# Moving the conversion of W_out between pairs of feed-forward steps

## The chip, the cores and the metric

The kernel runs on one core of a Trainium2 chip. The metric is the device time of one execution in microseconds (us). An engine is one of TensorE (PE, matmuls, with its weight loads shown apart as PEld), VectorE (DVE), ScalarE (ACT), GpSimd (POOL) and SyncE (SP, which issues nearly all DMAs). Each engine works through its own list of instructions in order and waits for the others at semaphores.

## The reference

Attention with a hashed mask, then a gated feed-forward; all in float32. Only the second half matters here.

```python
# attention: scores kept where the 6-bit hash buckets of query and key agree, softmax, times v
x = attn_out.transpose(0, 2, 1, 3).reshape(3072, 512)
h = x @ w_in                            # 3072 x 2048
g = h * (1.0 / (1.0 + np.exp(-1.702 * h)))
out = g @ w_out                         # 3072 x 512
```

The two weight matrices come to the kernel as 64-bit floats, so each is loaded as pairs of 32-bit words and turned into float32 on the chip ("converted").

## The kernel before, in words

**The work.** After the attention, `feed_forward` computes g for three blocks of 1024 tokens (the change's title calls a block a "token"; here it is "block 0, 1, 2") and writes g and sums of it to memory (`g_dram`); then it reads them back and multiplies by W_out. Both products are made by Strassen-Winograd recursion: seven products in place of eight, with sums on DVE and POOL. The first product has 8 steps per block, numbered n = 0 to 23, n = 8 * block + step. Steps 2 to 19 are taken in pairs t = 1 to 9 (`NESTED`), with n = 2t and 2t + 1. Pair 3 is the last of block 0, pairs 4 to 7 are block 1, pairs 8 and 9 are block 2.

**One pair.** `pair_of_steps` writes out the order by hand. PE runs ten full products of four matmuls of 512 columns (`product`, L743; p1, p6, p7, p5, p4, each for the first and the second step of the pair) and fourteen small ones of two matmuls of 256 columns (`small`, L817), two of the seven products being split a second time. The small ones are numbered go1, go6, go2, go7, go5, go4, go3, as their `go(i)` has it. PE's order in a pair is:

```
p1(0) go6' go2'  p1(1) go7'  p6(0) go5'  p6(1) go4'  p5(0) go3'
go1  p7(0) go6 go2  p7(1) go7  p5(1) go5  p4(0) go4  p4(1) go3   go1'
```

The marked ones belong to the split product 3, whose last six are carried over into the next pair. Small products use two places in PSUM: go1, go6, go7, go4 all go to place "a", go2, go5, go3 to place "x" (pool `inner`, one buffer each). DVE adds each result out of its place into u or v (L753, `u<-small` or `v<-small`), and PE may not write a place again before that. So go3 waits for DVE's addition of go5, go1' for that of go4, and go6' for that of go1'.

**What is put between.** `hook(1)` to `hook(10)` are places in that order where other work is issued: hook 6 stands ahead of p7(1), hook 7 ahead of p5(1), hook 8 ahead of p4(0), hook 9 ahead of p4(1), hook 10 at the end of the pair. `places_of` lists, for the two steps of a pair, the hooks that take their pieces of work; what is left over goes to hook 5 or 10.

**A conversion.** W_out comes in 16 chunks of 512 KB. `convert` does one chunk: a DMA into `raw` (L162, one buffer), then six DVE instructions of 128x512: L180, L182, L188, L193, L197, L200, with one on ACT (L190). They are six pieces: `todo[n]` holds six calls of `next(steps)`. After the fourth, L193, which reads `raw` last, `conversions` issues the DMA of the next chunk. It stands on SP's list behind the writes of g and its sums that were issued until then; SP goes through its list in order, and the writes wait for POOL's sums (L222 to L225, `g_outer`).

**Where the chunks lie.** `free` lists the steps that convert one chunk. Step 7 and step 15 have none, so pairs 3 and 7 convert one chunk each, at hooks 2 to 4; pairs 4 and 8 convert two chunks each, the first at hooks 2 to 7 and the second at hooks 7 to 10. DVE also computes sums of x for the next block (L222 to L225 with 128x1024 elements, `x_sums`): two in the last pair of a block, two in the first of the next one.

## Time and profile before

| what | value |
|---|---|
| median of 3 runs | 871.07 us (870.23 to 871.72) |
| the profiled execution | 870.98 us |
| its span, first to last instruction | 869.1 us |
| PE busy | 853.1 us, 98% of the span |
| DVE busy | 682.2 us, 78% |
| ACT, POOL busy | 340.8 us, 346.0 us |
| mean granted TensorE clock | 0.996 of full speed |

The span is that of the profiled execution; 1.9 us of its time lie outside it. "Busy" of PE counts matmuls that are pipelined, so 98% does not say that PE runs at its peak. The lists of instructions in order of time give start, length, engine, line, operation, tiles, and in brackets how long the engine had been idle and what released it.

### The profile page before, as it was taken

What the parts mean: (1) busy time and instruction counts of PE and PEld (TensorE: products, weight loads), DVE (VectorE), ACT (ScalarE), POOL (GpSimd) and SP (SyncE); (2) the same over time, 40 slices, a digit from 0 to 9 for tenths busy, and PEclk for the clock granted to TensorE, in tenths of its full rate; (3) what the DMA queues carried; (4) which work ended last, traced back from release to release, by engine and by line L of the source; (5) the groups of instructions that cost most, each with busy time, mean ns of one, the idle gap of its engine ahead of it and who ended that gap; (6) DMA issues with size and microseconds to landing.
All of it is one profiled execution on the core that took longest, in us unless ns stands there. A gap on an engine that the chain in (4) does not pass through costs nothing.

```text
span 869.1 us, 13717 instructions
## 1 busy us (share of the span) xinstructions
PE 853.1 (98%) x4953; PEld 520.4 (60%) x4953; DVE 682.2 (78%) x1032; ACT 340.8 (39%) x567; POOL 346.0 (40%) x322
## 2 busy tenths in 40 slices
PE   9999999999999999999899998999999999999996
PEld 5444444444444444555455554544888888888885
DVE  4589999999999885667676677756788977897786
ACT  5866667776666644334334433343000000000000
POOL 4242234333223569966633383779914100000000
PEclk9999999999999999999999999999999999999999
DMA  5636645445652104555445546568754685467524
GB/s 129 100 53 108 105 84 85 84 97 118 101 95 60 60 2 169 169 201 191 167 155 199 201 158 212 178 221 321 258 193 158 201 247 195 163 207 242 194 98 100
DMA packets 169164, 132.12 MB, mean 152 GB/s; under 512 B 123616, under 2 KB 138112, under 8 KB 163712
## 3 DMA queue, kind: packets, MB, share of 16 engines
q1 hardware_dynamic: 166528, 129.70, 52.3%
q10 hardware_dynamic: 2560, 1.46, 0.8%
q8 instruction: 41, 0.67, 0.4%
q14 instruction: 35, 0.29, 0.1%
HBM read 79.69 MB, written 50.33 MB: 150 GB/s over the span
## 4 chain that ended last, share of the span: by engine, by line
PE 85%; POOL 7%; issue 3%; DVE 3%; DMA 1%; ACT 0%; SPq 0%; ACTq 0%; POOLq 0%; DVEq 0%
PE product L1083 27%; PE product L743 18%; PE ps L435 18%; PE av L468 15%; PE small L817 4%; POOL t L224 1%; PE dn L489 1%; POOL t L222 1%; PE hash L411 1%; POOL v L223 1%; DMA raw<-in_moe_w_out_dram 1%; POOL t L225 1%; DVE xT L1087 1%; PE tp L369 1%; POOL xT L803 1%
## 5 line engine op out<-in xcount | busy, mean ns | idle before, releaser
L436 ACT ACTIVATE e<-ps 128x768 f32<-128x768 f32 x192 | 151.2, 812 | 25.7 <-PE ps L435 23.2
L435 PE MATMUL ps<-qT,kT 64*128 64x384 f32 x768 | 155.1, 482 | 0.0
L443 POOL TENSOR_TENSOR acc<-e 128x768 f32<-128x768 f32 x32 | 51.8, 1618 | 194.1 <-ACT e L436 174.6
L468 PE MATMUL av<-e,v 128*32 128x385 f32 x1536 | 128.0, 487 | 0.0
L743 PE MATMUL product<-xT,w_in_sb 128*128 128x512 f32 x216 | 101.7, 601 | 0.0
L468 PEld LDWEIGHTS av<-e,v 128*32 128x32 f32 x1536 | 48.6, 109 | 76.2 <-issue 74.5
L435 PEld LDWEIGHTS ps<-qT,kT 64*128 64x128 f32 x768 | 68.1, 188 | 38.5 <-issue 38.4
L743 PE MATMUL product<-t_x,s_in 128*128 128x512 f32 x192 | 89.1, 592 | 0.0
L1096 ACT COPY u<-product 128x256 f32<-128x256 f32 x21 | 7.8, 372 | 171.8 <-PE product L1083 138.6
L222 POOL TENSOR_TENSOR t<-v,u 128x512 f32<-128x512 f32 x24 | 33.3, 1387 | 87.1 <-ACT v L750 87.1
L435 PE MATMUL ps<-qf,kf 64*128 64x384 bf16 x384 | 62.9, 324 | 0.1
L743 PEld LDWEIGHTS product<-xT,w_in_sb 128*128 128x128 f32 x216 | 41.2, 192 | 36.2 <-issue 33.6
L444 POOL TENSOR_TENSOR acc<-acc,e 128x768 f32<-128x768 f32 x32 | 55.8, 1745 | 2.5
L743 PEld LDWEIGHTS product<-t_x,s_in 128*128 128x128 f32 x192 | 36.5, 190 | 30.9 <-issue 28.9
L449 DVE SCALAR_TENSOR_TENSOR acc<-e 128x768 f32<-128x768 f32 x32 | 47.7, 1490 | 5.1 <-ACT e L436 5.1
L753 DVE TENSOR_TENSOR v<-small,v 128x256 f32<-128x256 f32 x63 | 26.4, 421 | 30.7 <-PE small L817 30.5
L743 PE MATMUL product<-t_x,w_in_sb 128*128 128x512 f32 x96 | 45.2, 593 | 0.0
L435 PEld LDWEIGHTS <-kf 64*128 64x128 bf16 x384 | 18.9, 94 | 35.1 <-issue 6.2
L451 DVE TENSOR_TENSOR acc<-acc,e 128x768 f32<-128x768 f32 x32 | 34.3, 1072 | 3.3
L451 DVE TENSOR_TENSOR acc<-acc,acc 128x768 f32<-128x768 f32 x32 | 31.2, 974 | 6.3 <-POOL acc L444 3.2
L1083 PE MATMUL product<-raw_g,xT 128*128 128x256 f32 x152 | 35.1, 379 | 0.0
L225 POOL TENSOR_TENSOR t<-c,t 128x512 f32<-128x512 f32 x24 | 33.1, 1378 | 3.9 <-DMA g_dram<-t 2.2
(242 smaller groups left out, 1636.9 us busy)
## 6 DMA issues: line engine op xcount, KB each, us to landing
raw_g<-g_dram SPq DMA_DIRECT2D x22, 1024.0 KB
s_in<-g_dram SPq DMA_DIRECT2D x20, 1024.0 KB
g_dram<-t SPq DMA_DIRECT2D x72, 256.0 KB
g_dram<-c SPq DMA_DIRECT2D x48, 256.0 KB
raw<-in_moe_w_in_dram SPq DMA_DIRECT2D x16, 512.0 KB
raw<-in_moe_w_out_dram SPq DMA_DIRECT2D x16, 512.0 KB
v<-in_v_dram SPq DMA_DIRECT2D x32, 192.0 KB
g_dram<-u SPq DMA_DIRECT2D x24, 256.0 KB
```

The lines of the kernel that those rows point to most:

```text
L222: return [lambda: eng.tensor_tensor(t1, b12, b11, op=Alu.subtract), lambda: eng.tensor_tensor(b12, b22, b12, op=Alu.subtract), lambda: eng ...
L225: lambda: eng.tensor_tensor(t4, b21, t2, op=Alu.subtract)]
L435: nc.tensor.matmul(ps[:, j, 0:HS], a[hs, keys], m[hs, cols], start=not last, stop=last)
L436: nc.scalar.activation(es[c][:, kt, :, 0:HS], ps[:, :, 0:HS], Act.Exp, scale=1.0 / D**0.5)
L443: nc.gpsimd.tensor_tensor(acc, es[c][:, 0, :, 0:HS], es[c][:, 1, :, 0:HS], op=Alu.add)
L444: nc.gpsimd.tensor_tensor(acc, acc, es[c][:, 2, :, 0:HS], op=Alu.add)
L449: nc.vector.scalar_tensor_tensor(acc, e[0], T * TINY, e[1], op0=Alu.add, op1=Alu.add)
L451: nc.vector.tensor_tensor(acc, acc, x, op=Alu.add)
L468: nc.tensor.matmul(av[D * j + d : D * j + d + 32, :], vt[:, t, j, d : d + 32], es[c][:, t, j, :], start=(t == 0), stop=(t == T - 1))
L743: nc.tensor.matmul(ps, wq[LEFT[i]][:, kc, :], xq[RIGHT[i]][:, kc, :], start=(start and kc == 0), stop=(kc == K2 - 1), skip_group_check=not ...
L817: nc.tensor.matmul(ps[at], wq[LEFT[i]], xq[RIGHT[i]], start=start, stop=True, skip_group_check=not start)
L1083: nc.tensor.matmul(ps, wq[LEFT[i]][:, c, :], gq[RIGHT[i]][:, c, :], start=(c == 0), stop=(c == F4 - 1))
```

## The change

Steps 7 and 15 now convert a chunk, and steps 9 and 17 do not: pairs 3 and 7 convert two chunks, pairs 4 and 8 one. In pairs 4 and 8 the six pieces of the one chunk go to hooks 2, 4, 6, 7, 8, 9. In pairs 3 and 7 the first chunk keeps hooks 2, 2, 3, 3, 4, 4 and the second goes to hooks 6, 6, 6, 7, 9, 9. The order of the chunks and their number stay. A `get` is needed since step 17 has no list of its own any more.

```diff
-            free = [i for i in range(LATE + 1, 3 * MT) if i % MT != MT - 1]
+            free = [i for i in range(LATE + 1, 3 * MT) if i % MT != 1 or i < MT]
             for i in (list(range(1, LATE + 1)) if late else []) + free[:FC]:
                 todo[i] = [lambda: next(steps)] * 6
...
             for i, f in enumerate(low):
-                todo[first + i] = todo[first + i] + [f]
+                todo[first + i] = todo.get(first + i, []) + [f]
...
-                    places_of = (2, 4, 5, 6, 6, 7), (7, 8, 8, 9, 9, 10)
+                    places_of = (2, 4, 6, 7, 8, 9), ()
+                elif at == MT // 2 - 1:
+                    places_of = (2, 2, 3, 3, 4, 4), (6, 6, 6, 7, 9, 9)
                 else:
                     places_of = (2, 2, 3, 3, 4, 4), (6, 7, 7, 8, 9, 9)
```

## The prediction

> **What bounds the kernel now.** I read four views. First the page's list of engines and its chain that ended last: PE holds most of the chain.

> ```profile
> PE 853.1 (98%) x4953; PEld 520.4 (60%) x4953; DVE 682.2 (78%) x1032; ACT 340.8 (39%) x567; POOL 346.0 (40%) x322
> ...
> PE 85%; POOL 7%; issue 3%; DVE 3%; DMA 1%; ACT 0%; SPq 0%; ACTq 0%; POOLq 0%; DVEq 0%
> ```

> So only time in which PE stands still, or runs slowly, can be won. Second the waits of PE in the whole span; one of its three rows lies in the feed-forward:

> ```profile
> PE small L817 <- DVE u L753: 5.7, 4, 1.9
> ```

> Third, PE's instructions in order of time, to find these four waits (the columns: start, length, instruction, idle before). They are two in pair 4 and two in pair 8, at go3 and the go1' behind it. Pair 4:

> ```profile
> 428.46 1.88 PE L743 MATMUL product<-t_x,w_in_sb 128*128 128x512 f32 x4
> 432.26 0.70 PE L817 MATMUL small<-xT,w 128*128 128x256 f32 x2 [1.92 <-DVE u L753]
> 433.90 0.70 PE L817 MATMUL small<-xT,s_in 128*128 128x256 f32 x2 [0.95 <-DVE u L753]
> 434.44 3.37 PE L743 MATMUL product<-xT,w_in_sb 128*128 128x512 f32 x4
> 437.60 0.85 PE L817 MATMUL small<-xT,w 128*128 128x256 f32 x2
> 438.29 0.59 PE L817 MATMUL small<-xT,s_in 128*128 128x256 f32 x2
> 438.71 1.88 PE L743 MATMUL product<-xT,w_in_sb 128*128 128x512 f32 x4
> ```

> Elsewhere in these pairs, starts follow each other by 1.72 us behind a product of four matmuls and by 0.43 us behind a small one. Fourth, DVE in the same stretch, to see what it did instead:

> ```profile
> 424.96 1.05 DVE L200 SCALAR_TENSOR_TENSOR w_out_sb<-size,bits 128x512 f32<-128x512 f32 x1
> 429.99 0.69 DVE L180 TENSOR_SCALAR part<-raw 128x512 uint32<-128x512 uint32 x1 [3.99 <-DMA raw<-in_moe_w_out_dram]
> 430.59 0.68 DVE L753 TENSOR_TENSOR v<-product,v 128x512 f32<-128x512 f32 x1
> 431.19 0.68 DVE L753 TENSOR_TENSOR c<-product,c 128x512 f32<-128x512 f32 x1
> 431.79 0.41 DVE L753 TENSOR_TENSOR u<-small,u 128x256 f32<-128x256 f32 x1
> ...
> 433.44 0.41 DVE L753 TENSOR_TENSOR u<-small,u 128x256 f32<-128x256 f32 x1
> ```

> DVE, whose list is in order, stands for 3.99 us at the first instruction (L180) of the second chunk, since that chunk's load is under way; the sums of p5 and of go5, go4 are queued behind it, and PE's go3 and go1' wait for these. The load is late because SP issued it only at 425.49, behind POOL's writes:

> ```profile
> 425.01 0.38 SPq L747 DMA_DIRECT2D g_dram<-c  x1
> 425.49 0.40 SPq L162 DMA_DIRECT2D raw<-in_moe_w_out_dram  x1
> ```

> **What the two stalls cost.** Pair 4: from 428.46 to 438.71 PE started two products and four small ones, at the undisturbed spacing 2 * 1.72 + 4 * 0.43 = 5.16 us; it took 10.25, so 5.09 were lost. Part of it is the clock:

> ```profile
> 434.70:438.10 3.40, 3.40 (x6) 1.43 (x5) 2.09 (x4) 1.19 (x3) 0.00 (x0) 0.50 0.88 231
> ```

> In these 3.40 us the granted clock (third from the right) was 0.50, which cost 1.7 of the 5.09; waiting cost 3.4. Pair 8 has the same picture: DVE idles 3.96 us at L180 and the stretch from the product at 526.39 to the product at 532.35 took 5.96 us against 1.72 + 2 * 0.43 = 2.58; 3.38 lost, with the clock at 1.00.

> [...]

> **The change, part by part.**

> *Second chunk out of pairs 4 and 8.* No conversion now follows another in the pair, so nobody waits there for a load started in the pair. In the built order of pair 4, DVE has L188 after the sums of go6 and go2, L193 after that of go7, then p5's sums, go5's sum, L197, go4's sum, L200. With PE undisturbed: L188 at 423.30 (where L193 was), go7's sum at about 424.35 (PE ends go7 at 424.16, and sums start 0.2 later), L193 at 424.7, p5's sums at 426.14 and 426.74 (0.26 after p5 ends, as in pair 3), go5's sum at 427.34, done 427.75. PE wants go3 at 428.46 + 1.72 = 430.18: margin 2.4 us. L197 427.7, go4's sum 428.7 to 429.1, go1' wanted at 430.61: margin 1.5. The stalls go: -5.09 and -3.38 us. Bounds: none of it, if something else holds these sums; all of it at most, as PE can't run faster than its spacing. I take all, by the margins.

> *Second chunk into pairs 3 and 7.* Six DVE instructions move into a pair in which DVE was busy 15.76 of 23 us; 4.3 more make 20. What counts is DVE's order. From the rows of before, spacing is 0.71 us for a conversion step whose successor needs it, 0.61 otherwise, 0.78 for L197 ahead of L200, 0.90 for L200. Pair 3, from the sums of go6 and go2 (399.42, two of 0.33): L180 400.09, L182 400.80, L188 401.51, go7's sum 402.12 to 402.53 (go4 wants it at 404.82); L193 402.45, p5's sums 403.06 and 403.66, go5's sum 404.26. Before, these stood at 402.93, 403.54, 404.13: DVE filled an idle gap of 1.04 + 1.29 us and is only 0.13 later. Then L222 (1.92 to the next, as before) 404.6, go4's sum 406.51 to 406.92 (go1' wants it at 407.40), L197 406.84, L200 407.62, go3's sum 408.52, go1's sum 408.85 to 409.27. PE wants go6' at 409.55: margin 0.28 us, the smallest of all (before: done 408.46, 1.1). Behind it L224 from 409.2 to 410.8, go6''s sum done by 411.2, wanted by go7' at 412.13: 0.9. From the sum of go5' at 414.91, for which DVE waits anyway, all is as before. Cost: 0. It can't be a gain, since PE doesn't idle there. Upper bound: if each of the six steps took 0.79 and L200 1.07, their longest, they would need 0.7 more, 0.4 over the margin, in two pairs: +0.9. I take 0, the rows' middle.

> *Loads.* In pair 3 the first one is issued as before (393.53) and its 512 KB take 3.3 us with free DMA engines (524 KB moved from 394.4 to 396.8, and nothing after), 4.5 to 4.8 in traffic (425.49 to 429.97; 460.51 to 465.3). It is there by 398.3 at the latest, L180 wants it at 400.09: margin 1.8. The next is issued behind POOL's second L223, SP at about 405.8, there by 410.6, wanted at L180 at 413.4: 2.8. Pair 4's goes out behind the write of POOL's second L222, about 427.2, there by 432.0, wanted after go7' of the next pair at about 436: 4. Cost 0; were a load to take twice 4.8, the middle one would be 2.0 late and L180 end at 416.1; go5''s sum behind it, done by 416.5, is wanted by go3' at 418.57: still 0.

> *SP and POOL.* On SP the load passes two or three writes of g. They land up to 4.8 us later, and the rooms that they empty are wanted next a pair or nearly one later (POOL's L222 at 420.70 after a write issued at 407.6). The 1.05 and 1.12 us which POOL idles at L225 of pairs 4 and 8, waiting for a write behind the load, go; POOL then idles 17.1 us, so 0. On ACT L190 moves into an idle 0.60 us ahead of L864 (400.17 to 400.78): 0. PE's order is unchanged but for the names of the tiles; the sum of W_out (L214) in pair 8 ends at about 530.7, wanted at 533.27.

> **Sum.** The profiled execution took 870.98 us (span 869.1 and 1.9 outside), 0.09 under the median of 871.07. 870.98 - 5.09 - 3.38 = 862.5 us.

> **Rivals.**
> A. *A short wait at go6' in pairs 3 and 7*: DVE passes the margin of 0.28 by some tenths, up to the 0.9 above: 862.8 to 863.4. For it: two places with L222 and L224 stretched beside POOL (1.99 us against 1.22 of L214, of the same size). Against it: that stretch is counted already.
> B. *One pair keeps its stall*, since go5's sum is held by something that the trace of before hides behind L180: 870.98 - 5.09 = 865.9, or 867.6 if pair 8's is the one that goes. ACT's c (L864, 423.99 to 424.58) was there long before, POOL's too: little speaks for it.
> C. *Slower: the stall moves into pairs 3 and 7.* L180 of the second chunk stands at hook 6, ahead of the sums that go4, go3, go1' and go6' want. What the load is late beyond 400.09 + 0.28 goes straight to go6', with up to 1.7 for the clock. Slower than before needs 4.2 in each pair: 2.5 if the clock falls both times, thus a load of 9.4 us (393.53 to 402.9). At 12 us it would be 5.1 + 1.7 twice, 876 us. Against it: its longest shown landing is 4.8, and its neighbours on the queue are the same.
> D. *No change*: PE loses the same elsewhere later. PE has no other wait until the end (the waits list only these four), so 871 is unlikely.

> **Chances.** Forecast 0.80, A 0.07, B 0.05, C 0.06, D 0.02. The bound of what a measurement can tell is 0.2%, 1.7 us: faster are the forecast, A and B (0.92), same D (0.02), slower C (0.06). The range: below, the forecast less the 0.8 by which the three runs lie apart from their median, plus something for the clock at the start, 861.4; above, B's nearer end, 866.0. It leaves out about one in ten.

> **What would show it.** Right: L180 in pairs 4 and 8 without an idle of 4 us (waits of DVE on the load of W_out 11.3 us down to about 3); no wait of PE at go3 and go1'; the granted clock at 1.00 from 330 to 580; the stretch from one pair's p1(0) to the next 23.2 us for all pairs; L200 in pair 3 at about 407.6. Wrong: a wait of PE on DVE's v at go6' of pairs 3 and 7 (A), an idle of DVE at the L180 behind the sums of go6 and go2 there (C), or a wait left at go3 (B).

## The result, and the profile after

The changed kernel takes 862.25 us (median of 4 runs, 861.37 to 862.76) against 870.75 us of the kernel before (4 runs, 870.23 to 871.72): a ratio of 0.990 with a 95% interval of 0.9883 to 0.9917. The forecast was 862.5 us. The profiled execution took 861.94 us, its span is 860.1 us.

The page's chain that ended last, by engine, now consists of PE but for 2% of DVE, nearly all of it in the last 25 us of the kernel:

```profile
PE 97%; DVE 2%; issue 0%; ACTq 0%; ACT 0%; DVEq 0%
```

The list of PE's waits has one row left, at the very start of the kernel (who waited for whom: us in total, times, longest):

```profile
PE warm L362 <- DVE idle L76: 1.2, 1, 1.2
```

The end of pair 4 in PE's instructions in order of time, with p4(1), go3, go1', and p1(0) of the next pair. There is no bracket (no idle time) behind any of them, and they follow each other by 1.72 and 0.43 us:

```profile
427.94 1.88 PE L743 MATMUL product<-t_x,w_in_sb 128*128 128x512 f32 x4
429.66 0.59 PE L817 MATMUL small<-xT,w 128*128 128x256 f32 x2
430.09 0.59 PE L817 MATMUL small<-xT,s_in 128*128 128x256 f32 x2
430.52 1.88 PE L743 MATMUL product<-xT,w_in_sb 128*128 128x512 f32 x4
```

DVE in the same stretch: p5's two sums, go5's sum, L197, go4's sum, L200. No L180 stands ahead of them any more, and go5's sum is done at 427.23, 2.4 us before PE wants go3:

```profile
425.62 0.69 DVE L753 TENSOR_TENSOR v<-product,v 128x512 f32<-128x512 f32 x1 [0.75 <-POOL t L225]
426.23 0.68 DVE L753 TENSOR_TENSOR c<-product,c 128x512 f32<-128x512 f32 x1
426.82 0.41 DVE L753 TENSOR_TENSOR u<-small,u 128x256 f32<-128x256 f32 x1
427.16 0.68 DVE L197 TENSOR_TENSOR bits<-bits,part 128x512 f32<-128x512 f32 x1
428.14 0.42 DVE L753 TENSOR_TENSOR u<-small,u 128x256 f32<-128x256 f32 x1 [0.31 <-PE small L817]
428.48 1.06 DVE L200 SCALAR_TENSOR_TENSOR w_out_sb<-size,bits 128x512 f32<-128x512 f32 x1
```

The conversions now stand in pair 3, between the sums that PE wants there. This is the stretch of DVE in which the prediction had its smallest margin (L222 is the sum of x with 1024 elements; the last line is the sum of go1', for which go6' waits):

```profile
399.57 0.68 DVE L180 TENSOR_SCALAR part<-raw 128x512 uint32<-128x512 uint32 x1
...
404.07 1.90 DVE L222 TENSOR_TENSOR t_x<-xT 128x1024 f32<-128x1024 f32 x1
405.89 0.41 DVE L753 TENSOR_TENSOR u<-small,u 128x256 f32<-128x256 f32 x1
406.23 0.67 DVE L197 TENSOR_TENSOR bits<-bits,part 128x512 f32<-128x512 f32 x1
406.93 1.07 DVE L200 SCALAR_TENSOR_TENSOR w_out_sb<-size,bits 128x512 f32<-128x512 f32 x1
407.85 0.41 DVE L753 TENSOR_TENSOR u<-small,u 128x256 f32<-128x256 f32 x1
408.17 0.41 DVE L753 TENSOR_TENSOR v<-small,v 128x256 f32<-128x256 f32 x1
```

The sum of go1' ends at 408.58 and PE starts go6' at 409.03 as its spacing wants: 0.45 us to spare. By stretches of one pair (PE, PEld, DVE, ACT, POOL busy, then the granted clock), pairs 3 and 4 look like this:

```profile
384.10:407.30 23.20, 23.20 (x69) 12.92 (x68) 17.14 (x31) 9.31 (x16) 13.57 (x17) 1.00 0.62 206
407.30:430.50 23.20, 23.20 (x69) 12.92 (x68) 17.44 (x29) 9.18 (x16) 19.56 (x17) 1.00 0.54 191
```

Each takes 23.2 us with the clock at full speed, and DVE's work is now shared evenly, 17.1 and 17.4 us.

The two profiled spans differ by 9.0 us. At p1(0) of pair 3, before the first instruction that the change moves, the changed kernel is already 0.52 us ahead (384.10 against 384.62), and it is still 0.52 ahead at p1(0) of pair 4 (407.31 against 407.83). The profiles below that have no stall in pair 3 reach the latter anywhere from 407.2 to 407.8, so this part differs from execution to execution. Between there and the first product behind pair 9 (546.57 against 555.56) lie 139.26 us in place of 147.73: the 8.47 us are the 5.09 + 3.38 of the two stalls.

### The profile page after: what moved, and what is told of

Read it like the earlier page. It is cut to its first block, busy times and chain, and to the rows that moved or that the text cites. A ratio compares the mean times of both kernels' runs of the same rounds, so it can differ in the third digit from the quotient of the medians.

```text
span 860.1 us, 13716 instructions
## 1 busy us (share of the span) xinstructions
PE 850.0 (99%) x4953; PEld 519.2 (60%) x4953; DVE 682.0 (79%) x1032; ACT 341.3 (40%) x567; POOL 346.3 (40%) x322
## 4 chain that ended last, share of the span: by engine, by line
PE 97%; DVE 2%; issue 0%; ACTq 0%; ACT 0%; DVEq 0%
PE product L1083 28%; PE product L743 26%; PE ps L435 18%; PE av L468 15%; PE small L817 6%; PE dn L489 1%; PE hash L411 1%; DVE xT L1087 1%; PE tp L369 1%; DVE y L1063 1%; PE warm L362 0%; PE hash L376 0%; DVE v L1087 0%; DVE t2a L224 0%; DVE raw_g L223 0%
## 5 line engine op out<-in xcount | busy, mean ns | idle before, releaser
L743 PE MATMUL product<-xT,w_in_sb 128*128 128x512 f32 x216 | 100.2, 593 | 0.0
L743 PE MATMUL product<-t_x,s_in 128*128 128x512 f32 x192 | 89.1, 592 | 0.0
L222 POOL TENSOR_TENSOR t<-v,u 128x512 f32<-128x512 f32 x24 | 33.4, 1390 | 80.4 <-ACT v L750 80.4
L743 PEld LDWEIGHTS product<-xT,w_in_sb 128*128 128x128 f32 x216 | 40.9, 190 | 35.8 <-issue 33.2
L743 PEld LDWEIGHTS product<-t_x,s_in 128*128 128x128 f32 x192 | 36.5, 190 | 31.0 <-issue 28.9
L753 DVE TENSOR_TENSOR v<-small,v 128x256 f32<-128x256 f32 x63 | 26.2, 420 | 30.6 <-PE small L817 30.2
L743 PE MATMUL product<-t_x,w_in_sb 128*128 128x512 f32 x96 | 45.2, 593 | 0.0
L753 DVE TENSOR_TENSOR c<-product,c 128x512 f32<-128x512 f32 x24 | 16.5, 686 | 22.1 <-issue 8.6
```

Source lines behind the costliest of these rows:

```text
L222: return [lambda: eng.tensor_tensor(t1, b12, b11, op=Alu.subtract), lambda: eng.tensor_tensor(b12, b22, b12, op=Alu.subtract), lambda: eng ...
L743: nc.tensor.matmul(ps, wq[LEFT[i]][:, kc, :], xq[RIGHT[i]][:, kc, :], start=(start and kc == 0), stop=(kc == K2 - 1), skip_group_check=not ...
L753: nc.vector.tensor_tensor(dst, x, y, op=Alu.add)
```

## The experiments

The theory is that of the prediction: DVE stood at L180 for a load that was issued too late, and the sums behind it held PE. The main rival is that two conversions beside the sums of x are simply too much work for DVE in one pair.

### The second chunk loaded ahead, conversions left in place

The kernel before, with its conversions in their places. Only the second chunk of pairs 4 and 8 is loaded into another room (buffer in SBUF), and so a pair earlier.

```diff
...
+                room = w_out_sb[:, 0:2, 12:16, :]...            # rows that are converted last
+                ahead = (7, 14) if late else ()                  # second chunks of pairs 4 and 8
-                gens = [convert(cv, *x, psum=psum) for x in chunks]
+                gens = [convert(cv, *x, psum=psum, raw=room if i in ahead else None) for i, x in enumerate(chunks)]
...
+                        if at == 3 and i + 2 in ahead:
+                            src = chunks[i + 2][1].rearrange("f (h x) two -> f h x two", h=2)
+                            for h in range(2):
+                                loader[0].dma_start(out=room[:, h], in_=src[:, h])
```

> The kernel before, with its two conversions in pairs 4 and 8 as they were; only the second chunk of each is loaded long ahead, into rows of w_out_sb that are not written yet, in place of the one room that the first chunk still occupies. If the loss is DVE standing at L180 for a load issued too late, both stalls go without moving a conversion: 870.75 - 5.1 - 3.4 = 862.3 us, and DVE has no idle of 4 us at L180. If the rival holds, that two conversions beside the sums of x are too much work for DVE in such a pair, the waits of PE at go3 and go1' stay and the time is 870 to 871 us.

Measured: 862.86 us (861.75 to 863.37), ratio 0.9892, interval 0.9867 to 0.9917; the profiled one 861.75. PE has no wait in the feed-forward. DVE in pair 4 of this run, in order of time (its lines stand five further down: L185 is L180, L205 is L200, L758 the sums). The second chunk starts straight behind the first, with no idle:

```profile
424.41 1.05 DVE L205 SCALAR_TENSOR_TENSOR w_out_sb<-size,bits 128x512 f32<-128x512 f32 x1
425.30 0.75 DVE L185 TENSOR_SCALAR part<-w_out_sb 128x512 uint32<-128x512 uint32 x1
...
427.14 0.42 DVE L758 TENSOR_TENSOR u<-small,u 128x256 f32<-128x256 f32 x1
```

So twelve conversion steps do fit into pair 4; the late load was the whole loss. The change wins by moving the second chunk to where its load has landed, not by relieving DVE. Loading ahead is as good as far as these runs can tell (the medians are 0.6 us apart, and the runs of the two overlap), but it needs a second room.

### One half of the change at a time

Pairs 3 and 4 alone, then pairs 7 and 8 alone. For the first (the second has 7 and 17 for 9 and 15, and `t == 8`, `t == 7`):

```diff
-            free = [i for i in range(LATE + 1, 3 * MT) if i % MT != 1 or i < MT]
+            free = [i for i in range(LATE + 1, 3 * MT) if i != 9 and i != 15 and i != 23]
...
-                    places_of = (2, 4, 6, 7, 8, 9), ()
-                elif at == MT // 2 - 1:
+                    places_of = ((2, 4, 6, 7, 8, 9), ()) if t == 4 else ((2, 4, 5, 6, 6, 7), (7, 8, 8, 9, 9, 10))
+                elif t == 3:
```

> The change in pairs 3 and 4 alone; pairs 7 and 8 as before. If the two stalls are separate and each goes with its own pair, what is left is pair 8's: 862.25 + 3.4 = 865.7 us, or 867.4 if the granted clock halves behind it. If the gain were of one piece (say, a shift that the second pair needs too), 862 or 871.

> The change in pairs 7 and 8 alone; pairs 3 and 4 as before. What is left is pair 4's stall: 3.4 us of waiting, 865.7 us, or 867.4 if the granted clock halves behind it. Both this run and the one for pairs 3 and 4 between 865.5 and 867.5 would mean that the waits add up.

Measured: 867.29 us (865.31 to 868.42), ratio 0.9944, 0.9924 to 0.9963; and 867.73 us (866.98 to 868.52), ratio 0.9944, 0.9926 to 0.9962. Each half brings about half, though the second lies 0.2 us above the 867.5 that was expected at most. PE's two waits at the end of pair 8 in the run with pairs 3 and 4 alone:

```profile
520.95 1.88 PE L743 MATMUL product<-t_x,w_in_sb 128*128 128x512 f32 x4
524.60 0.70 PE L817 MATMUL small<-xT,w 128*128 128x256 f32 x2 [1.78 <-DVE u L753]
526.25 0.70 PE L817 MATMUL small<-xT,s_in 128*128 128x256 f32 x2 [0.95 <-DVE u L753]
526.78 1.88 PE L743 MATMUL product<-xT,w_in_sb 128*128 128x512 f32 x4
```

Between the two products lie 5.83 us against 2.58: 3.25 lost, no slow matmul behind it. At the end of pair 4 in the run with pairs 7 and 8 alone:

```profile
427.92 1.88 PE L743 MATMUL product<-t_x,w_in_sb 128*128 128x512 f32 x4
431.91 0.70 PE L817 MATMUL small<-xT,w 128*128 128x256 f32 x2 [2.11 <-DVE u L753]
433.56 1.22 PE L817 MATMUL small<-xT,s_in 128*128 128x256 f32 x2 [0.95 <-DVE u L753]
434.57 3.05 PE L743 MATMUL product<-xT,w_in_sb 128*128 128x512 f32 x4
...
438.33 1.88 PE L743 MATMUL product<-xT,w_in_sb 128*128 128x512 f32 x4
```

10.41 us against 5.16: 5.25 lost, with the clock at half for one stretch. The spans are 863.5 and 865.3; 860.1 + 3.25 and 860.1 + 5.25 make 863.4 and 865.4. The stalls are separate and add up.

### The kernel before once more

> The kernel before, unchanged, to see in another execution whether the halved clock belongs to pair 4. If it hangs on where a window of 3.4 us falls, it can stand at either stall, at both or at none: 869.3, 870.9 or 872.6 us by 1.7 us each; waiting itself stays 3.4 us in each pair. If pair 4 has it always, 870.9.

Measured: 871.26 us (870.25 to 873.97), ratio 0.9994, 0.9978 to 1.0011. In this profiled execution the clock fell behind both stalls: from 427.86 to the p1(1) at 438.01, 10.15 us against 5.16, and in pair 8, which lost 3.38 us in the first profile:

```profile
525.69 1.88 PE L743 MATMUL product<-t_x,w_in_sb 128*128 128x512 f32 x4
529.42 0.70 PE L817 MATMUL small<-xT,w 128*128 128x256 f32 x2 [1.85 <-DVE u L753]
531.06 0.70 PE L817 MATMUL small<-xT,s_in 128*128 128x256 f32 x2 [0.94 <-DVE u L753]
531.60 3.17 PE L743 MATMUL product<-xT,w_in_sb 128*128 128x512 f32 x4
...
535.87 1.88 PE L743 MATMUL product<-xT,w_in_sb 128*128 128x512 f32 x4
```

10.18 us against 5.16, 5.02 lost. The waits are as long as before, only the clock differs. So the halved clock does not belong to pair 4 alone. Four profiles hold six such stalls: pair 4's was followed by a slow stretch in all three of its cases, pair 8's in one of three.

### The places in pairs 3 and 7

The second chunk there at the hooks that any other pair uses.

```diff
-                elif at == MT // 2 - 1:
-                    places_of = (2, 2, 3, 3, 4, 4), (6, 6, 6, 7, 9, 9)
```

> The changed kernel, but the second chunk of pairs 3 and 7 at the hooks of any other pair: 6, 7, 7, 8, 9, 9 for 6, 6, 6, 7, 9, 9. L193 then stands behind p5's and go5's sums, ahead of L222. From the rows of after, go1's sum would end at 409.06 in its time, go6' is wanted at 409.03: a wait of PE at go6' of 0 to 0.3 us in each of the two pairs, 862.3 to 862.9 us. If the places there don't matter, 862.25 and no wait; if DVE has no room at all there, 1 us or more in each.

Measured: 861.97 us (861.38 to 863.38), ratio 0.9894, 0.9878 to 0.9911, and no wait of PE in the feed-forward. DVE at L222 in pair 3 of this run:

```profile
404.75 1.43 DVE L222 TENSOR_TENSOR t_x<-xT 128x1024 f32<-128x1024 f32 x1
```

The expectation had the margin at go6' used up; it is 0.37 us (the sum of go1' ends at 408.86, go6' starts at 409.23), since L222 came 0.5 us later, counted from p1(0) of pair 4 in each run, but took 1.43 us for 1.90. The special list of places for pairs 3 and 7 is worth nothing that these runs can tell.

### The one chunk of pairs 4 and 8, packed

```diff
-                    places_of = (2, 4, 6, 7, 8, 9), ()
+                    places_of = (2, 2, 3, 3, 4, 4), ()
```

> The changed kernel, but the one chunk of pairs 4 and 8 at hooks 2, 2, 3, 3, 4, 4 for 2, 4, 6, 7, 8, 9. If taking the second chunk away is all that matters, 862.25 us. By the rows of after, L188, L193, L197, L200 then stand ahead of go4', go3' and go1's sums: go1's sum ends at about 421.0 and PE wants go6 at 420.63, so 0.4 us in each pair, 863.1 us. If spreading carries the gain, several us.

Measured: 863.65 us (862.79 to 864.84), ratio 0.9911, 0.9895 to 0.9927. PE's instructions in pair 4 of this run; the waiting one is go6, as expected, and the same stands in pair 8 with 0.36:

```profile
419.29 1.88 PE L743 MATMUL product<-xT,w_in_sb 128*128 128x512 f32 x4
421.55 0.67 PE L817 MATMUL small<-xT,w 128*128 128x256 f32 x2 [0.37 <-DVE u L753]
...
422.48 1.88 PE L743 MATMUL product<-xT,w_in_sb 128*128 128x512 f32 x4
```

Between the products lie 3.19 us against 2.58, 0.6 lost in each pair (0.4 was expected). So spreading the remaining chunk carries about 1.2 us of the gain, by the trace; taking the second chunk away carries the rest.

### The second chunk loaded late

The second chunk of pairs 3 and 7 is loaded two or three times into the same room.

```diff
-        (queue or loader[0]).dma_start(out=raw, in_=src)
+        for _ in range(loads):                    # 2 or 3 for these two chunks, else 1
+            (queue or loader[0]).dma_start(out=raw, in_=src)
```

> The changed kernel, but the second chunk of pairs 3 and 7 is loaded three times over into the same room, the third load behind three writes of g on SP's list, so that it lands at about 405 to 406 in place of 396.5. L180 is wanted at 399.57; what is late passes to PE's go4 and go6' but for the margin of 0.45: a wait of 5 to 6 us in each of the pairs, 872.5 to 874 us, and up to 1.7 more for each halved window, 876. If DVE has slack behind hook 6, less: 862 to 868.

> As the run with three loads, with two: the second lands at 400 to 401, up to 1.6 us after L180 wants it at 399.57. Waits of PE at go6' of 0 to 1.2 us in each of the pairs 3 and 7: 862.3 to 864.6 us, without a halved clock.

Measured: three loads, 873.67 us (872.37 to 874.47), ratio 1.0021, 1.0006 to 1.0036, where 872.5 to 874 was expected; two loads, 862.49 us (862.14 to 863.08), ratio 0.9899, 0.988 to 0.9919. With three, DVE in pair 3 (lines one further down, L181 is L180) stands as in pair 4 of the kernel before:

```profile
405.69 0.69 DVE L181 TENSOR_SCALAR part<-raw 128x512 uint32<-128x512 uint32 x1 [6.07 <-DMA raw<-in_moe_w_out_dram]
```

and PE in the same place waits at go4, then is slow:

```profile
402.55 1.88 PE L744 MATMUL product<-t_x,w_in_sb 128*128 128x512 f32 x4
408.21 0.70 PE L818 MATMUL small<-w_out_sb,w_in_sb 128*128 128x256 f32 x2 [3.78 <-DVE u L754]
408.75 2.80 PE L744 MATMUL product<-t_x,w_in_sb 128*128 128x512 f32 x4
...
413.15 1.88 PE L744 MATMUL product<-xT,w_in_sb 128*128 128x512 f32 x4
```

From p4(0) to the next pair's p1(0) it took 10.60 us against 4.73: 5.87 lost in pair 3. In pair 7, from p4(0) to the next pair's p1(1) (501.26 to 513.67), it took 12.41 against 7.31: 5.10 lost, with the clock at 1.00 and DVE idle for 5.72 at its L181. The place of the loss is where rival C of the prediction had it, and with this load the change is no gain: its median is a little above that of the kernel before. With two loads L180 came 0.51 us late in pair 3 and 0.32 in pair 7 by DVE's idle, and PE did not wait in the feed-forward. In pair 3:

```profile
400.59 0.69 DVE L181 TENSOR_SCALAR part<-raw 128x512 uint32<-128x512 uint32 x1 [0.51 <-DMA raw<-in_moe_w_out_dram]
```

### DVE made late by work

L180 of the second chunk in pairs 3 and 7 is executed twice, or four times.

```diff
-            nc.vector.tensor_scalar(part, hi, 3, 0x3FFFFFFF, ...)
+            for _ in range(1 + extra):            # 1 or 3 for these two chunks, else 0
+                nc.vector.tensor_scalar(part, hi, 3, 0x3FFFFFFF, ...)
```

> The changed kernel with L180 of the second chunk in pairs 3 and 7 done twice over (the result is the same), which puts 0.7 us of DVE work ahead of L222. If DVE's lateness passes straight on to PE's go6', as the prediction has it, 0.7 less the 0.45 of margin that the trace of after shows: a wait of 0.25 us in each pair, 862.8 us. If L222's end is set by the end of POOL's second L223 (1.08 us after it in four runs, whenever L222 starts), the 0.7 go into L222's own wait: L222 at 404.8 lasts 1.2 instead of 1.90, no wait of PE, 862.25 us.

> As with one more L180, but three more, 2.1 us of DVE work. If lateness passes straight on: 2.1 - 0.45, a wait of 1.7 us in each of the two pairs, 865.6 us. If L222 waits for whichever POOL instruction is under way: L222 reaches the front at 406.2, POOL's L224 has ended about then, L222 ends at 407.3 in place of 405.97, so go4's and go1's sums are 1.3 late: a wait of about 0.9 in each, 864.0 us.

Measured: one more, 862.53 us (861.90 to 862.93), ratio 0.9886, 0.9854 to 0.9919, no wait of PE in the feed-forward; three more, 866.86 us (866.32 to 866.98), ratio 0.9934, 0.9911 to 0.9958. L222 is L223 in these runs. With one more, DVE's sum of x in order of time:

```profile
405.24 1.21 DVE L223 TENSOR_TENSOR t_x<-xT 128x1024 f32<-128x1024 f32 x1
```

and POOL's instructions beside it in the same run:

```profile
404.06 1.27 POOL L224 TENSOR_TENSOR v<-c,v 128x512 f32<-128x512 f32 x1
405.29 2.29 POOL L225 TENSOR_TENSOR t<-c,t 128x512 f32<-128x512 f32 x1
```

0.7 us of work more and L222 0.7 shorter: it ends as it would have. The time alone (862.25 or 862.8 expected) does not separate the two rules, these rows do. With three more, the same line of DVE:

```profile
406.62 2.28 DVE L223 TENSOR_TENSOR t_x<-xT 128x1024 f32<-128x1024 f32 x1
```

and the POOL instruction that was under way:

```profile
406.55 1.27 POOL L226 TENSOR_TENSOR t<-c,t 128x512 f32<-128x512 f32 x1
```

Here DVE came 0.07 us after POOL's next instruction had begun; that one ended at 407.82, and L222 1.08 later, at 408.90. PE then waited 1.78 us at go1' in pair 3 and 1.82 in pair 7. Neither number of the expectation came out (864.0 and 865.6 against 866.9), and that of the first rule, by which lateness passes straight on, was the nearer one. The rows speak for the second: counted from p4(0) of each run, L222 started 2.2 us later than in the changed kernel and ended 2.6 later, 1.08 behind a POOL instruction; the expectation had it start ahead of that instruction.

## Why the prediction was right, point by point

- **What bounds the kernel, and the two stalls.** Right. The waits at go3 and go1' are gone, the load ahead removes them without moving a conversion, and one half of the change removes one of them.
- **Their sizes, 5.09 and 3.38 us.** Right for the profiled execution, 8.47 us of difference between the two traces from pair 4 on. As a property of the pairs they were not: 5.09 and 3.38 differ by the slow stretch behind the first. Pair 8 shows waiting alone, 3.25 and 3.38; pair 4 was never seen without a slow stretch, and less 1.7 for it the three cases leave 3.3 to 3.6.
- **Why the load was late.** Right in part. L193 gives the room free at 423.98; SP's order puts the issue off to 425.49, 1.5 us, but L180 starts only at 429.99. The other 4.5 us, from the issue to L180, are the landing.
- **Pair 4 after the change.** The order on DVE came out as worked, within 0.1 us of each time once the earlier start of 0.52 us is taken off; the margin of 2.4 us at go3 was measured as 2.4.
- **Cost of the chunk in pairs 3 and 7, taken as 0.** Right. The margin at go6' was 0.45 us, not 0.28, and rival A did not come about. About 0.1 of the difference is L222, whose end did not move with its start, and 0.08 is L197, with 0.70 to L200 in place of 0.78. The busy time was read from a stretch that is no pair: 15.76 us belong to 396 to 419, where it became 19.4. Pair 3 itself, from p1(0) to p1(0), went from 14.1 to 17.1.
- **"What the load is late ... goes straight to go6'" (rival C).** This step failed. Half a microsecond (two loads) and 0.7 us (one more L180) went nowhere: L222 ended 1.08 to 1.12 us after POOL's second L223 had ended, whether DVE reached it 0.8 us or 0.1 us before. The spare time there is about 0.8 us by which L222 gets shorter and 0.45 behind it, until DVE misses the gap, as with three more L180. Rival C's direction and place hold, with three loads: 873.67 us, and of the 5.72 us that DVE stood idle in pair 7, 5.10 reached PE. Rivals B and D did not come about: no wait is left at go3, and PE has none elsewhere.
- **The order of the places in pairs 3 and 7** was worked out instruction by instruction, but another order gives the same time. The places in pairs 4 and 8 mattered more (0.6 us in each pair), which the prediction didn't price.
- **Loads, SP, POOL, ACT: 0.** Nothing in the trace speaks against it. DVE waits 3.7 us in all for loads of W_out, 2.32 of it at 355.25, outside these pairs; about 3 were expected.
- **The clock.** Right for the changed kernel: it stood at 1.00 from 330 to 580. Behind pair 8's stall it fell to 0.50 in one profile of three, behind pair 4's in three of three, and what decides on it was not shown (the last section has the numbers). With one behind each stall the kernel before was expected to take 872.6 us, but it also took up to 875.4.
- **The time.** 862.5 forecast, 862.25 measured. The mechanism carries the 8.47; agreement to 0.25 us is in part luck, as executions of one kernel differ by 0.5 us before pair 3 already.

## What to carry to other kernels

A wait on the engine that bounds the kernel can come from a load two steps back, as here: follow it from PE's bracket to the engine that it names, and from there to the one instruction with a long idle and a DMA behind it. With a single room for loaded data, the second of two users in a row paid the whole landing time here, 4.5 us; either give it a room of its own, or put other work between them. Before counting a late instruction as lost, look whether the next one on that engine ends with a neighbour's work anyway, and how wide the gap is that it must meet: here 0.7 us of lateness cost nothing, 2.1 us made PE wait for 1.8.

## What the runs showed of the hardware that was not expected

**DVE's sum ended at a fixed distance behind POOL's instruction.** L222 (two inputs in SBUF, 128x1024) took from 1.21 to 2.28 us in pair 3 of these seven runs, but in all of them it ended 1.08 to 1.12 us after the end of the POOL instruction that was under way when it started:

| run | L222 starts | that POOL instruction ends | L222 ends |
|---|---|---|---|
| before | 404.46 | 405.37 | 406.45 |
| after | 404.07 | 404.89 | 405.97 |
| old places | 404.75 | 405.09 | 406.18 |
| two loads | 405.11 | 405.32 | 406.40 |
| one more L180 | 405.24 | 405.33 | 406.45 |
| three more L180 | 406.62 | 407.82 | 408.90 |
| three loads | 410.20 | 410.83 | 411.91 |

And the POOL instruction that came next lasted 2.25 to 2.29 us for 1.27 in the first five, the 1 us of L222 longer, and 1.70 or 1.71 for 0.73 in the last two, where it is a shorter one. Why the two change length, the runs do not show. The conversion steps, which read at most one operand from SBUF, kept their 0.67 to 0.70 us beside POOL (L200 its 1.03 to 1.07).

What makes the clock fall stays open. In the 3.41 us just ahead of each of the four slow stretches PE was busy, by the profile, for 0.70, 0.80, 1.50 and 1.67 us, so it was idle all through in none of them. In pair 8 of the first profile it was busy for 0.70 us from 528.30 to 531.71, and in pair 7 with three loads it stood idle for 3.43 us ahead of go4, both without a slow stretch behind. So how long PE stands idle does not sort the cases, and whether the place of a stall among the multiples of 3.413 does was not shown.

A slow stretch cost 1.7 us in pair 4 of the first profile, half of its 3.41, since PE was busy all through it (3.40 of 3.40 us). It cost less, by the author's estimate, where PE would have waited anyway: with three loads pair 3 had one and lost only 0.8 us more than pair 7, which waited 1.01 us at go1' instead, and part of that for a later load. The six runs with pairs 3 and 4 alone lie at 865.3 to 865.4 us with a mean clock of 0.997, at 867.2 to 867.4 with 0.995 to 0.996, and at 868.4 with 0.992: which would be none, one and probably more slow stretches, but only the profiled run (865.42, without) shows where the clock stood. And 11 of the 40 runs of the kernel before that stand beside the experiments took 873.6 to 875.4 us at a mean clock of 0.989 to 0.992, against 0.994 to 0.996 for the others. Two slow stretches of 1.7 us do not make these times; no profile caught such a run, and where their clock fell is not shown.
